# Stacking the high and low parts of a value sum into one 128-partition tile, with one-layer T blocks in 64x128 pairs and filler matmuls

## The chip, the cores and the metric

The kernel runs on one core of one Trainium2 chip. The metric is the device time in microseconds (us), lower is better. Most executions of a kernel agree within 0.3%.

## The reference, cut to what matters

A block A is a recurrent attention: 64 segments of 32 tokens, and 8 memory rows that each segment hands to the next. A block B is a gated feed-forward layer. The model is A, B, A, B with the same weights both times.

```python
for s in range(n_seg):                                   # 64 segments, one after another
    h = concat([mem, xs])                                # 8 memory rows + 32 tokens = 40 rows of 448
    q, k, v = h @ Wq, h @ Wk, h @ Wv                     # 16 heads of 256
    p = softmax(where(mask, q @ k.T / 16, -1e9))
    o = sum_over_heads((p @ v) @ Wo)
    mem = o[:8]                                          # the next segment waits for this
    outs.append(o[8:])
...
x = x + A(layernorm(x)); x = x + B(layernorm(x))         # twice
```

## The kernel before

The kernel folds Wq with Wk and Wv with Wo, so that a segment is: T = M h (the "T blocks"), scores, softmax, U = h p, and the value sum N U. The two A layers run side by side, the second four steps behind the first: steps 0 to 3 and 64 to 67 have one layer (40 columns), steps 4 to 63 have two (80 columns). The memory rows go first through every stage: `s_mem` (scores of the memory rows), `p_t_mem` (transpose of their probabilities, tile Pm), `u_mem` (tile UTm), `un_mem` (value sum, 56 matmuls of 448 columns), `m_t` and `m_nat` (the new memory, selected out of the sum). `s_seg`, `u_seg` and `un` do the same for the 32 tokens, `b_layer` and `b_down` are the block B. A list scheduler with tuned numbers (`SLOT`, `BIAS`) puts all operations in order before the kernel is built.

`un_mem` leaves four partial sums, one in each quarter of 32 partitions. The sum over the quarters and the choice of rows are done by one matmul with a 0/1 matrix. The matmul takes bf16, so the sum is split into a high and a low part, each multiplied by the same matrix:

```python
# un_mem, after its 56 matmuls into the PSUM bank C
S.act(... S.hi[:, :] = C)                                 # bf16
S.dve(... S.lo[:, :] = C - S.hi)
# m_t: the new memory, transposed; 4 column blocks x (hi, lo) = 8 matmuls
[MM(C.b()[:, c*16:c*16+16], x[:, w:w+128], S.selm[...], start=(i == 0), stop=(i == 1))
 for c, w in ((0, 0), (1, 128), (2, 256), (3, 320)) for i, x in enumerate((S.hi, S.lo))]
# m_nat: the same in natural layout; 2 matmuls of 448 columns
[MM(C.b()[:, 0:D], S.seln[:, w, :], x[:, :], start=(i == 0), stop=(i == 1)) for i, x in enumerate((S.hi, S.lo))]
```

The first part of each T block has a contraction of 64 rows. It is done in quads of 64x64 matmuls that run side by side (`mode=3`), 25 quads a step:

```python
for o, x in ((0, a), (0, b), (1, a), (1, b)):             # 4 matmuls of 64x64
    h, g = slice(64*side, 64*side+64), slice(64*o, 64*o+64)
    out.append(MM(R[x].b()[g, j*n:j*n+n], S.M3[h, slot, g], mov(3, h), start=(j == 0), stop=False))
```

Of the kernel before, what the change touches and what calls it, by code (L numbers as in the profile page):

```python
# [44 lines left out]
class _Sched:  # L45
# [118 lines left out]
    "t_block@a": 1812, "t_blockm+": -9357, "t_blocks+": -8, "s_mem+": -142986, "p_t_mem@a": 31328, "p_t_mem+": -7192,  # L164
    "u_mem@a": 13521, "u_mem+": 747, "un_mem@a": -12628, "un_mem+": -15687, "un_memh+": -12449, "m_t@a": 6986,
    "m_t+": 6465, "m_tk+": -7932, "s_seg@a": 8100, "s_seg+": -15857, "seg_pt+": -131, "u_seg@a": 3317,
    "u_seg0+": -34358, "u_seg1+": -19122, "u_seg2+": 20412, "u_seg3+": 10778, "m_nat@a": 16787, "m_nat+": 67952,
    "t_block0f+": 11522, "t_block0r+": -14766, "t_block1r+": 16356, "ln_a+": 2229, "ln_ac+": -36153, "un@a": 57889,
    "un+": -5801, "ln_b+": -22707, "b_layer@a": -6365, "b_layer+": 479, "b_down@a": -28772, "b_down+": -16128,
    "m_natx+": 65420, "m_nat@z": -27634, "s_mem@z": 9161, "p_t_mem@z": -19432, "u_mem@z": -334, "un_mem@z": 8381,  # L170
    "m_t@z": 18252, "s_seg@z": -4933, "u_seg@z": 6743, "un@z": -14160, "b_layer@z": 39068, "b_down@z": -1631,
    "seg_pt@z": -26944, "ln_b@z": 196, "stay": 33066, "win": 142,
# [5 lines left out]
    "t_block0f.0@0": 23150, "t_block0r.0@0": 20466, "t_block0r.1@0": 10373, "t_block0r.2@0": -118963,  # L178
    "t_block0r.3@0": -102813, "t_block0r.4@0": -15176, "t_block0r.5@0": 95232, "t_block1f.0@0": 88326,
    "t_block1r.0@0": 70572, "t_block1r.1@0": -90708, "t_block1r.2@0": -669, "t_block1r.3@0": 23477,  # L180
    "t_block2r.0@0": 105637, "s_mem.0@0": -153732, "p_t_mem.0@0": -26811, "u_mem.0@0": -7044, "un_mem.0@0": 68017,
    "m_t.0@0": -385871, "s_seg.0@0": 180805, "u_seg0.0@0": 16616, "u_seg1.0@0": -3087, "u_seg2.0@0": 182854,
    "u_seg3.0@0": -7016, "m_nat.0@1": 15351, "t_block0f.0@1": -101435, "t_block0r.0@1": 175650,
    "t_block0r.1@1": -16550, "t_block0r.2@1": -78417, "t_block0r.3@1": -96693, "t_block0r.4@1": -96697,
    "t_block0r.5@1": -76748, "t_block1f.0@1": 94756, "t_block1r.0@1": -93576, "t_block1r.1@1": -61388,
    "t_block1r.2@1": 13060, "t_block1r.3@1": 192482, "t_block2r.0@1": 98249, "s_mem.0@1": 6005,
    "p_t_mem.0@1": -100695, "u_mem.0@1": 172343, "un_mem.0@1": 413220, "m_t.0@1": 76060, "s_seg.0@1": 89640,
    "u_seg0.0@1": 96587, "u_seg1.0@1": -148969, "u_seg2.0@1": 71131, "u_seg3.0@1": -99947, "un0.0@1": 269897,
    "un0.1@1": -174852, "un0.2@1": 156565, "un0.3@1": -89383, "un1.0@1": 70834, "un1.1@1": 69072, "un1.2@1": -29917,
    "un1.3@1": 26881, "un2.0@1": -89787, "un2.1@1": -86447, "un2.2@1": -10845, "un2.3@1": 13517, "un3.0@1": 89653,  # L190
    "un3.1@1": 89684, "b_layerf.0@1": 94811, "b_layer.0@1": 48867, "b_layer.1@1": 96741, "b_layerf.1@1": 109098,
    "b_layer.2@1": -3240, "b_layer.3@1": 70642, "b_down.0@1": 354372, "b_down.1@1": 72900, "b_down.2@1": 254015,
    "b_down.3@1": 240246, "b_down.4@1": 326259, "b_down.5@1": 354136, "b_down.6@1": 78849, "m_nat.0@2": 168132,
    "t_block0f.0@2": -10118, "t_block0r.0@2": -98052, "t_block0r.1@2": -41109, "t_block0r.2@2": 66134,
    "t_block0r.3@2": 13073, "t_block0r.4@2": -14618, "t_block0r.5@2": -188807, "t_block1f.0@2": -3221,
    "t_block1r.0@2": -1996, "t_block1r.1@2": -186700, "t_block1r.2@2": 70640, "t_block1r.3@2": -74211,
    "t_block2r.0@2": 16205, "s_mem.0@2": -92464, "p_t_mem.0@2": -20075, "u_mem.0@2": -252353, "un_mem.0@2": -101434,
    "m_t.0@2": 84256, "s_seg.0@2": 96377, "u_seg0.0@2": 90135, "u_seg1.0@2": 97804, "u_seg2.0@2": 182858,
    "u_seg3.0@2": 260389, "m_nat.0@3": 151329, "t_block0f.0@3": -2977, "t_block0r.0@3": -188538,
    "t_block0r.1@3": 75914, "t_block0r.2@3": -96292, "t_block0r.3@3": 6194, "t_block0r.4@3": -75085,  # L200
    "t_block0r.5@3": 69297, "t_block1f.0@3": -185930, "t_block1r.0@3": 111423, "t_block1r.1@3": -36939,
    "t_block1r.2@3": 10926, "t_block1r.3@3": 370, "t_block2r.0@3": 12228, "s_mem.0@3": -124071, "p_t_mem.0@3": 180760,
    "u_mem.0@3": 6506, "un_mem.0@3": 65274, "m_t.0@3": -389, "s_seg.0@3": -12148, "u_seg0.0@3": -75151,
    "u_seg1.0@3": 176089, "u_seg2.0@3": 78879, "u_seg3.0@3": 340369, "un0.0@3": -161383, "un0.1@3": -95386,
    "un0.2@3": 323286, "un0.3@3": 5996, "un1.0@3": 11452, "un1.1@3": 76963, "un1.2@3": -93171, "un1.3@3": -179086,
    "un2.0@3": 162572, "un2.1@3": -2533, "un2.2@3": -15402, "un2.3@3": 334269, "un3.0@3": -77062, "un3.1@3": 94056,
    "b_layerf.0@3": 350365, "b_layer.0@3": 277881, "b_layer.1@3": 268897, "b_layerf.1@3": 354905,
    "b_layer.2@3": 181729, "b_layer.3@3": 192495, "b_down.0@3": 101118, "b_down.1@3": 346959, "b_down.2@3": -2948,
    "b_down.3@3": -287771, "b_down.4@3": 93426, "b_down.5@3": 159732, "b_down.6@3": 83157, "m_nat.0@0": -484,
    "un0.4@3": -268098, "un0.5@3": -13365, "un0.6@3": 248971, "un0.7@3": -102719, "un1.4@3": 260089, "un1.5@3": -4388,  # L210
    "un1.6@3": -67736, "un1.7@3": -9258, "un2.4@3": 265064, "un2.5@3": 334268, "un2.6@3": 332162, "un2.7@3": 163179,
    "un3.2@3": 8603, "un3.3@3": -7565, "b_layer.4@3": -10753, "b_layer.5@3": 79668, "b_layer.6@3": 131945,
    "b_layer.7@3": 253283, "b_layer.4@1": 182601, "b_layer.5@1": 61111, "b_layer.6@1": 10905, "b_layer.7@1": -174890,
    "seg_pt.0@3": -162209, "un.0@3": 195399, "ln_b.0@1": 303926,
# [3 lines left out]
def bias_keys(o):  # L218
    if not o.cat:
        return []  # L220
    if o.kind != "pe":
        return [o.cat + o.sub + "+"]
    return [o.cat + "@a"] if o.t < LAG else [o.cat + "@z"] if o.t >= NSEG else []
# [19 lines left out]
class _Order:  # L243
# [13 lines left out]
    def add(self, kind, eng, cost, fn, rd, wr, name=None, mode=0, lat=None, alt=None, base=(0, 0)):  # L257
        o = _Op()
        o.kind, o.eng, o.cost, o.fn, o.rd, o.wr, o.name, o.mode = kind, eng, cost, fn, list(rd), list(wr), name, mode
        o.alt, o.base = alt, base  # L260
        o.succs, o.np, o.alloc, o.fixed, o.lat, o.cat, o.sub, o.t = [], 0, [], None, lat, self.cat, self.sub, self.t
        o.slot = None
        if kind == "pe" and o.cat:
            name = o.cat + o.sub
            i = self.count[name] = self.count.get(name, -1) + 1
            o.slot = f"{name}.{i}@{o.t % 4}"
        self.ops.append(o)
        return o
# [195 lines left out]
def MM(out, lhsT, rhs, **kw):  # L464
    return (out, lhsT, rhs, kw)


class _Kernel:
# [16 lines left out]
    def alloc(self):  # L485
# [37 lines left out]
        self.lo = self.sb("lo", [128, D])  # L523
        self.ident = self.sb("ident", [128, 128])
# [369 lines left out]
    def warm(self, n, rd, wr):  # L894

        S = self
        T = S.tile("R", 1)
        S.mm(lambda: [MM(T.b()[:, 0:512], S.ident[:, :], S.N[:, 0:2, 0:256], start=True, stop=True) for _ in range(n)], n * S.pitch(512), rd, T.res() + wr)
# [6 lines left out]
    def t_block(self, t, units):  # L905
# [14 lines left out]
        def first():  # L920
            out = []
            for a, b in zip(range(0, len(units), 2), range(1, len(units), 2)):
                for j in range(units[a][2]):
                    for o, x in ((0, a), (0, b), (1, a), (1, b)):
                        c, u0, m = units[x]
                        side, slot = S.PLACE[16 * c + u0 + j]
                        h, g = slice(64 * side, 64 * side + 64), slice(64 * o, 64 * o + 64)
# [3 lines left out]
        if pair:  # L931
            S.mm(first, sum(u[2] for u in units[::2]) * S.pitch(n) + 25.0, rd, [r for x in R for r in x.res()] + [k for u in units for k in keys(*u)], mode=3)
# [46 lines left out]
    def s_mem(self, t):  # L979
# [7 lines left out]
             [("TTm",) + k for k in S.TKEYS] + [("hTx", pp, s, l) for l in range(l0, l1)] + S.mkeys(pp, s, l0, l1), C.res())  # L987
# [13 lines left out]
    def s_seg(self, t):  # L1001
# [5 lines left out]
        def mms():  # L1007
            b = G.b()
            out = []
            for l in range(l0, l1):  # L1010
# [9 lines left out]
             [("mask", 0), ("TTsz", 0), ("TTsz", 1)] + S.mkeys(pp, s, l0, l1), G.res())  # L1020
# [19 lines left out]
    def seg_pt(self, t):  # L1040
        S = self
        if t == NSTEP - 1:

            T = S.pe_transpose([("Ps",)], lambda a: S.Ps[:, a, :], [("PTs",)])
# [5 lines left out]
    def p_t_mem(self, t):  # L1050
# [3 lines left out]
        S.mm(lambda: [MM(pT()[:, 0:128], S.Pm[:, :], S.ident[:, :], is_transpose=True)], 60.0, [("Pm",), ("ident",)], C.res() + [("PTm",)])  # L1054
# [12 lines left out]
    def u_mem(self, t):  # L1067
# [6 lines left out]
             [r for l in C for r in C[l].res()] + [("UTm", S.win(t), l) for l in C], mode=3)  # L1074
# [291 lines left out]
```

## Time and profile before

| | before |
|---|---|
| time | 1564.83 us, median of 3 runs (1560.64 to 1566.0) |
| TensorE busy | 96% of the span |
| steps 0 to 3 with the setup, up to the last matmul of their last `un_mem` | 141.7 us |
| steps 4 to 7 | 80.6 us |
| steps 8 to 63, called the middle: 14 periods of four steps | 1236.3 us |
| the rest, called the end | 105.3 us |

From the page of the profiled execution: the span, the busy time of each engine, the clock that TensorE was granted in 40 slices (9 is 90% or more), and the queue that brings instructions (packets, MB, share).

```profile
span 1563.9 us, 81992 instructions
...
PE 1505.9 (96%) x37969; PEld 1106.3 (71%) x37969; DVE 868.0 (56%) x2353; ACT 858.3 (55%) x2599; POOL 112.0 (7%) x259
...
PEclk9989999999999999999999999999999999999998
...
q8 instruction: 298, 4.88, 1.3%
```

The table of the four stretches (length, busy time of each engine with its number of instructions, granted clock, DMA share, GB/s):

```profile
0.00:141.70 141.70, 109.87 (x2060) 64.58 (x2064) 75.43 (x261) 69.72 (x214) 18.96 (x34) 0.93 0.62 147
141.70:222.30 80.60, 76.32 (x2270) 57.10 (x2264) 45.12 (x122) 46.20 (x144) 6.00 (x15) 1.00 0.09 18
222.30:1458.60 1236.30, 1224.48 (x31145) 919.97 (x31136) 696.47 (x1821) 705.36 (x2116) 81.15 (x196) 1.00 0.09 18
1458.60:1563.90 105.30, 95.21 (x2513) 64.61 (x2505) 51.01 (x150) 37.02 (x127) 5.86 (x14) 0.94 0.09 16
```

In the middle TensorE is busy 1224.5 of 1236.3 us at full clock. The two ends have idle time and a clock below 1. What TensorE waited for from 216 to 1440 us, which is the window of all such tables of the middle below (total us, times, longest):

```profile
PE b L138 <- ACT big L798: 4.9, 14, 0.4
PE b L138 <- DVE UTm L799: 3.4, 13, 0.3
PE b L138 <- issue: 2.6, 5, 1.1
```

"issue" is time in which the engine waited for nothing that the profile shows. The timeline of TensorE around one `un_mem` of every fourth step (start, us, engine, line, operation, count, idle before it):

```profile
305.82 0.22 PE L138 MATMUL b<-ident,Pm 128*128 128x128 bf16 x1
305.87 0.92 PE L138 MATMUL b<-big,hB 128*128 128x448 bf16 x4
306.72 0.39 PE L138 MATMUL b<-PTm,hK 40*64 40x128 bf16 x16
307.05 0.55 PE L138 MATMUL b<-big,hB 128*128 128x448 bf16 x2
307.86 2.83 PE L138 MATMUL b<-Nw,UTm 128*32 128x448 bf16 x56 [0.26 <-DVE UTm L799]
```

Between the products for the memory (PTm) and `un_mem` (UTm) two copies of 0.6 us have to happen. They run side by side, one on ScalarE and one on VectorE (307.17 to 307.80 us). Two `b_down` matmuls cover most of that; the rest is the 0.26 us of waiting. The selection of one step (start, us, engine, line, operation, count):

```profile
579.13 0.17 PE L138 MATMUL b<-selm,hi 128*128 128x16 bf16 x1
579.16 0.17 PE L138 MATMUL b<-selm,lo 128*128 128x16 bf16 x1
...
579.52 0.35 PE L138 MATMUL b<-lo,seln 128*128 128x448 bf16 x1
579.71 2.43 PE L138 MATMUL b<-Nw,big 128*128 128x448 bf16 x12
```

The starts show the cost: eight selm matmuls from 579.13 to 579.34 (0.21 us), two seln matmuls from 579.34 to 579.71 (0.37 us). In half of the steps each of these matmuls is cut into four quarters (128x32); there the selection is 32 + 8 matmuls.

### The profile page before, as it was taken

The page shows a single profiled execution, that of the slowest core. Times are in us where ns is not written, and L with a number is a line of the kernel's source. Part 1 is how long each engine was busy: PE and PEld are TensorE (multiplying, and loading weights), DVE is VectorE, ACT ScalarE, POOL GpSimd, SP SyncE. Part 2 cuts the span into 40 slices and gives each one's busy share as a digit, 9 for nine tenths or more (in the row PEclk, how much of TensorE's full clock was granted, in tenths as well). Part 3 has the DMA queues.
Part 4 walks back from the last instruction along what each step waited for, and adds up shares of the span by engine and source line. Part 5 has one row for each costly group of instructions (what it writes and reads, how often), then busy time and mean ns, then how long its engine had stood idle before and what let it go on. Part 6 is the DMA issues. An engine that isn't in the chain of part 4 may idle for free.

```text
span 1563.9 us, 81992 instructions
## 1 busy us (share of the span) xinstructions
PE 1505.9 (96%) x37969; PEld 1106.3 (71%) x37969; DVE 868.0 (56%) x2353; ACT 858.3 (55%) x2599; POOL 112.0 (7%) x259
## 2 busy tenths in 40 slices
PE   5889999999999999999999999999999999999997
PEld 2457667777677777777677777777677777777665
DVE  7434565655555655555555655555564655555554
ACT  5734555655555565655555565555555555555432
POOL 4000000000000000000000000000000000000000
PEclk9989999999999999999999999999999999999998
DMA  8841001000010100000011100101010100000000
GB/s 182 205 117 35 19 18 20 18 17 16 20 20 12 25 15 20 17 15 20 16 20 15 24 15 16 19 16 21 16 21 14 22 18 15 15 18 19 15 19 14
DMA packets 129735, 46.01 MB, mean 29 GB/s; under 512 B 117736, under 2 KB 129264, under 8 KB 129392
## 3 DMA queue, kind: packets, MB, share of 16 engines
q1 hardware_dynamic: 129040, 40.53, 12.4%
q8 instruction: 298, 4.88, 1.3%
q14 instruction: 45, 0.37, 0.1%
q10 hardware_dynamic: 352, 0.24, 0.1%
HBM read 10.33 MB, written 1.84 MB: 8 GB/s over the span
## 4 chain that ended last, share of the span: by engine, by line
PE 92%; DVE 3%; SPq 2%; ACT 2%; issue 1%; DMA 1%; POOL 0%; POOLq 0%; DVEq 0%
PE b L138 92%; SPq L622 2%; ACT hi L1096 1%; ACT big L798 1%; DVE UTm L799 1%; DMA Nw<-in_A_Wo_dram 0%; DVE selm L658 0%; DMA PTs<-Ps 0%; DVE seln L661 0%; DVE stat L845 0%; DVE part L1192 0%; DVE lo L1097 0%; ACT UTm L798 0%; DVE big L799 0%; DVE xn L852 0%
## 5 line engine op out<-in xcount | busy, mean ns | idle before, releaser
L138 PE MATMUL b<-hT,Mw 128*128 128x80 bf16 (+1 forms) x11424 | 436.7, 200 | 9.2 <-issue 8.6
L138 PEld LDWEIGHTS b<-hT,Mw 128*128 128x128 bf16 x11424 | 415.3, 100 | 22.7 <-issue 14.3
L138 PE MATMUL b<-Nw,big 128*32 128x448 bf16 (+1 forms) x3540 | 295.1, 356 | 1.8 <-DVE big L799 0.8
L798 ACT ACTIVATE TTs<-b 128x320 bf16<-128x320 f32 (+5 forms) x658 | 278.4, 426 | 3.7 <-PE b L138 3.7
L798 ACT ACTIVATE TTm<-b 128x80 bf16<-128x80 f32 (+5 forms) x658 | 153.2, 235 | 137.7 <-PE b L138 131.9
L138 PEld LDWEIGHTS b<-Nw,big 128*32 128x32 bf16 (+1 forms) x3540 | 136.4, 97 | 108.8 <-issue 2.4
L138 PE MATMUL b<-xBT,big 128*128 128x128 bf16 (+3 forms) x4900 | 208.7, 215 | 0.7 <-ACT xBT L798 0.7
L138 PEld LDWEIGHTS b<-xBT,big 128*128 128x128 bf16 (+1 forms) x4900 | 187.6, 102 | 19.3 <-issue 7.1
L138 PE MATMUL b<-Nw,UTm 128*32 128x448 bf16 x3752 | 193.5, 358 | 5.3 <-DVE UTm L799 3.6
L138 PEld LDWEIGHTS b<-Nw,UTm 128*32 128x32 bf16 x3752 | 97.2, 98 | 91.2 <-DVE UTm L799 10.0
L798 ACT ACTIVATE big<-b 128x512 bf16<-128x512 f32 (+1 forms) x258 | 128.5, 560 | 35.2 <-PE b L138 35.0
L799 DVE CAST TTm<-b 64x64 bf16<-64x64 f32 (+4 forms) x226 | 48.6, 216 | 176.3 <-PE b L138 174.7
L138 PE MATMUL b<-hT,M 64*64 64x80 bf16 (+2 forms) x7208 | 142.8, 198 | 2.0 <-DVE M L799 1.2
L138 PEld LDWEIGHTS b<-hT,M 64*64 64x64 bf16 (+1 forms) x7208 | 110.9, 108 | 28.0 <-ACT hT L798 7.1
L799 POOL COPY hK<-xn 32x448 bf16<-32x448 bf16 x136 | 75.1, 552 | 657.3 <-DVE xn L852 651.0
L798 ACT ACTIVATE UTm<-b 128x512 bf16<-128x512 f32 (+1 forms) x144 | 78.3, 567 | 74.3 <-PE b L138 74.3
L1263 ACT ACTIVATE gT<-b 128x512 bf16<-128x512 f32 (+2 forms) x128 | 69.4, 542 | 62.1 <-PE b L138 50.2
L138 PE MATMUL b<-big,hB 128*128 128x448 bf16 (+1 forms) x574 | 100.1, 354 | 0.7 <-DVE hB L1264 0.7
L1264 DVE TENSOR_TENSOR hB<-gT,b 128x512 bf16<-128x512 bf16 (+2 forms) x128 | 79.3, 619 | 38.1 <-ACT gT L1263 21.8
L798 ACT ACTIVATE hT<-b 64x16 bf16<-64x16 f32 (+1 forms) x134 | 24.0, 179 | 125.9 <-DVE hT L799 88.0
L799 DVE CAST TTs<-b 64x256 bf16<-64x256 f32 (+4 forms) x226 | 90.5, 401 | 2.7 <-PE b L138 2.6
L1096 ACT ACTIVATE hi<-b 128x448 bf16<-128x448 f32 x67 | 36.5, 544 | 91.6 <-PE b L138 91.6
(112 smaller groups left out, 1625.4 us busy)
## 6 DMA issues: line engine op xcount, KB each, us to landing
big<-in_A_Wo_dram SPq DMA_DIRECT2D x3, 896.0 KB, 6.0
out_dram<-ys SPq DMA_DIRECT2D x32, 56.0 KB, 2.0
big<-in_B_W_up_dram SPq DMA_DIRECT2D x7, 224.0 KB, 2.9
big<-in_B_W_gate_dram SPq DMA_DIRECT2D x7, 224.0 KB, 3.3
big<-in_B_W_down_dram SPq DMA_DIRECT2D x7, 224.0 KB, 2.6
XA<-in_A_x_dram SPq DMA_DIRECT2D x28, 56.0 KB, 2.3
PTs<-Ps SPq DMA_TRANSPOSE x67, 2.4
Nw<-in_A_Wo_dram SPq DMA_DIRECT2D x1, 896.0 KB, 6.1
```

Source lines behind the costliest of these rows:

```text
L138: ins = E.matmul(out, lhsT=lhsT, rhs=rhs, **kw)
L622: S.q.add("dma", ("sp",), {"sp": 6200.0 if w == "Wv" and q else 4100.0}, lambda E: E.dma_start_transpose(out=st[w, q], in_=src[w][:, q * 1 ...
L798: return E.activation(out(), src(), ACT.Copy)
L799: return E.tensor_copy(out(), src())
L1096: S.act(lambda E: E.activation(S.hi[:, :], C.b()[:, 0:D], ACT.Copy), D, C.res(), [("hi",)])
L1263: S.act(lambda E, g=g, R=R, n=n: E.activation(S.gT[:, g, 0:n], R[0].b()[:, 0:n], ACT.Relu), n, R[0].res(), [("gT", g)])
L1264: S.dve(lambda E, g=g, R=R, n=n, fcs=fcs: E.tensor_tensor(S.hB[:, fcs[0]:fcs[-1] + 1, 0:w], S.gT[:, g, 0:n].rearrange("p (a b) -> p a b", ...
```

## The change

Three things, and with them a new tuning of the scheduler:

1. In the steps with two layers, the quarters are added in pairs first (64 partitions), and high and low then stand in one tile of 128 partitions. The selection matrix has the same rows four times, so one pass sums both: half the selection matmuls.
2. In the steps with one layer, two 64x128 matmuls replace each quad of 64x64 (the code says so; the change's own short name speaks of 128x64).
3. Filler matmuls on constant data in the softmax gaps of steps 0, 1 and 67, so that the clock doesn't fall.

```diff
+        if S.stacked(t):                                   # LAG <= t < NSEG: steps 4 to 63
+            S.cp(sumA[:, :] <- C.b()[64:128, 0:D], eng=("act",))
+            S.dve(sumB = C.b()[0:64, 0:D] + sumA)
+            S.cp(S.hi[0:64, :] <- sumB, eng=("act",))
+            S.dve(S.hi[64:128, :] = sumB - S.hi[0:64, :])
+            return
         S.act(... S.hi[:, :] = C)
         S.dve(... S.lo[:, :] = C - S.hi)
 ...
-  for i, x in enumerate((S.hi, S.lo))                      # m_t and m_nat
+  for i, x in enumerate(S.parts(t))                        # (hi,) where stacked
 ...
-                    for o, x in ((0, a), (0, b), (1, a), (1, b)):
+                    for o, x in ((0, a), (0, b), (1, a), (1, b)) if l1 - l0 == 2 else ((-1, a), (-1, b)):
 ...
+    def fill(self, t, n):
+        if t < 2 or t == NSTEP - 1:
+            for _ in range(n):
+                S.warm(2, [("gap", t)], [("filled", t)])    # 2 matmuls of 512 columns
 ...
-    "t_blockm+": -9357, "s_mem+": -142986, ...              # BIAS and SLOT, all new;
-            o.slot = f"{name}.{i}@{o.t % 4}"                # the first and last steps have slots of their own
+            o.slot = f"{name}.{i}@" + (f"a{o.t}" if o.t < LAG else f"z{o.t - NSEG}" if o.t >= NSEG else str(o.t % 4))
```

The new tuning also puts products of the value weights into the softmax gaps of step 0.

## The prediction

> **What bounds it now.** TensorE. The page gives it 96% of the span busy, DVE 56%, ACT 55%; the chain of waits puts 92% on the matmul line. The middle repeats every four steps: in the chain un_mem begins at 307.86, 395.85, 483.82 us, a period of 88.0 us, and the table by stretches shows PE busy 87.4 of 88.0 us at clock 1.00. Some periods have short "issue" gaps (0.3 to 1.1 us); the mean of fourteen is 88.3. The two ends are different: clock 0.81, 0.83, 0.62 in 79 to 107 us and 0.80 after 1536; un_mem takes 4.1 and 5.25 us there against 2.86; and PE waits on softmax (1.08 us, twice) and on "issue" (1.49, 1.38, 0.70, 0.82, 0.84).
>
> **Removed in the middle.** The PE timeline shows the hi/lo selection as 0.21 us (selm) plus 0.37 us (seln) per step. Stacking halves both: about 0.29 us per step, 60 steps, 17.5 us. A mode change costs 95 ns (131 ns start to start against 36); the built order has 744 of them against 796, part of that in the ends. The Trainium skill (TensorEngine Tiling, Key Properties) says that a mode change drains the array; the trace agrees. Summing the built order with start-to-start times of the trace, I estimate 1.4 us less PE work per period.
>
> **Added.** Hi/lo is now ACT, DVE, ACT, DVE instead of ACT, DVE: with 0.54 and 0.62 us each, un_mem's end to the selection goes from about 1.5 to about 2.75 us. The new order puts 2.8 to 3.3 us of other PE work there (before: 1.3 to 4.5), so the latency is just hidden; I allow 0.2 us per period for short stalls where ACT or DVE is in use. The added 1.2 us per step is off the critical chain. Net: 88.3 to about 87.0, fourteen periods, about 17 us.
>
> **Ends.** One-layer T blocks: a quad of 64x64 tiles with 40 columns takes 32 ns, a pair of 64x128 perhaps 28, so about 1 us directly; 400 fewer matmuls should also shorten the issue gaps. Fillers and value-weight products moved into the softmax gaps of steps 0 and 1 keep the clock up. The Trainium skill (TensorE: Matmul & The Clock Gate, Part 1) gives windows of 3.4 us that halve the clock after idleness; the clock column agrees. At full clock un_mem of steps 0 and 1 saves 3.6 us, the last steps about 4. Eighteen more filler matmuls cost 3.9 us, mostly in idle time. I expect about 8 us at the start and 6 at the end, less certain than the middle.
>
> **Sum.** 17 + 8 + 6, rounded down: 1535 us, range 1524 to 1549. Faster by over 2% (below 1533.5) 0.45, within 2% 0.52, slower 0.03.
>
> **Right or wrong, by the profile.** Period 86.7 to 87.4 us, every selection one pass (selm about 0.11, seln 0.19 us); no wait of PE on the lo operation above 0.3 us in the middle; un_mem of steps 0 and 1 near 2.9 us; clock about 1.0 in the first steps and near 1536; ACT and DVE up by about 33 to 37 us each, harmless.
>
> **What would make it wrong.** ACT or DVE queues late at the longer chain, so that PE waits 0.5 us or more per step and the middle gains nothing; PSUM banks held longer because the sum reads them through two engines; fillers that run at half clock and delay the transposes behind them; issue gaps that don't shrink, or that come elsewhere since instruction supply is the limit.

## The result

| | before | after |
|---|---|---|
| time, median | 1562.74 us (4 runs, 1558.9 to 1566.0) | 1542.06 us (4 runs, 1540.84 to 1542.92) |
| ratio | | 0.9868, 95% interval 0.9841 to 0.9895 |
| setup and steps 0 to 3 | 141.7 | 124.8 |
| steps 4 to 7 | 80.6 | 89.6 |
| middle | 1236.3 | 1231.0 |
| end | 105.3 | 95.4 |

A ratio is the mean time of one kernel's runs over that of the other's of the same rounds, so it is not quite the ratio of the medians. The change is worth 1.3%, inside the 2% that count as "the same". The stretches are read from the two traces (spans 1563.9 and 1540.8 us). The page after:

```profile
span 1540.8 us, 79677 instructions
...
PE 1478.4 (96%) x36772; PEld 1084.9 (70%) x36777; DVE 919.9 (60%) x2445; ACT 882.9 (57%) x2627; POOL 111.8 (7%) x259
...
q8 instruction: 288, 4.72, 1.3%
```

The four stretches after:

```profile
0.00:124.80 124.80, 102.83 (x1893) 62.13 (x1900) 75.39 (x267) 67.88 (x208) 19.04 (x34) 1.00 0.73 167
124.80:214.40 89.60, 81.06 (x2263) 61.10 (x2255) 49.13 (x134) 46.77 (x143) 8.50 (x20) 0.92 0.09 18
214.40:1445.40 1231.00, 1206.23 (x30360) 899.45 (x30352) 743.66 (x1888) 732.01 (x2156) 78.58 (x191) 1.00 0.08 18
1445.40:1540.80 95.40, 88.28 (x2276) 62.27 (x2270) 51.72 (x158) 36.24 (x121) 5.71 (x14) 1.00 0.08 17
```

Read the third line against its twin before: TensorE's busy time in the middle fell by 18.3 us (1224.5 to 1206.2), about the 1.4 us a period (19.6 us) that was predicted for the removed work, but the middle became only 5.3 us shorter. So 13 us of removed work turned into waiting (idle time 11.8 before, 24.8 us after). The waits of TensorE in the middle name it:

```profile
PE b L138 <- ACT UTm L865: 15.8, 13, 1.2
PE b L138 <- DVE big L866: 5.1, 14, 0.4
```

The wait of `un_mem` for UTm grew from 3.4 to 15.8 us, once in every period, 1.2 us each time (a fourteenth lies just past the window). The timeline around one of them, with ScalarE (ACT) and VectorE (DVE):

```profile
559.40 1.67 PE L138 MATMUL b<-big,hB 128*128 128x448 bf16 x8
561.04 0.23 PE L138 MATMUL b<-ident,Pm 128*128 128x128 bf16 x1
561.10 0.54 PE L138 MATMUL b<-big,hB 128*128 128x448 bf16 x2
561.57 0.41 PE L138 MATMUL b<-PTs,hK 40*64 40x512 bf16 x4
561.81 0.37 PE L138 MATMUL b<-PTm,hK 40*64 40x128 bf16 x16
562.01 0.39 PE L138 MATMUL b<-PTs,hK 40*64 40x512 bf16 x4
562.03 1.52 ACT L865 ACTIVATE UTm<-b 128x512 bf16<-128x512 f32 x3 [0.46 <-PE b L138]
...
563.61 2.83 PE L138 MATMUL b<-Nw,UTm 128*32 128x448 bf16 x56 [1.21 <-ACT UTm L865]
```

In the new order two products of the previous segment (PTs) stand on TensorE just around the memory's product (PTm). Their copies and the memory's copy all go into the tile UTm, three of them on ScalarE, one behind the other from 562.03 to 563.55. `un_mem` reads UTm, so it waits for the third. (The memory's other copy is on VectorE and was done at 562.95.) Before, `b_down` matmuls stood there, and each engine had one copy to make.

The selection after is one pass, as intended: four selm matmuls in 0.10 us (16 quarters in one step of four), one seln matmul of about 0.19 us:

```profile
570.10 0.25 PE L138 MATMUL b<-selm,hi 128*128 128x16 bf16 x4
...
570.58 0.35 PE L138 MATMUL b<-hi,seln 128*128 128x448 bf16 x1
```

### The profile page after: what moved, and what is told of

It is laid out like the page before. It is cut to its first block, busy times and chain, and to the rows that moved or that the text cites. A ratio compares the mean times of both kernels' runs of the same rounds, so it can differ in the third digit from the quotient of the medians.

```text
span 1540.8 us, 79677 instructions
## 1 busy us (share of the span) xinstructions
PE 1478.4 (96%) x36772; PEld 1084.9 (70%) x36777; DVE 919.9 (60%) x2445; ACT 882.9 (57%) x2627; POOL 111.8 (7%) x259
## 4 chain that ended last, share of the span: by engine, by line
PE 87%; DVE 6%; ACT 4%; DMA 2%; issue 1%; POOL 0%; POOLq 0%
PE b L138 87%; DMA xBT<-xn 2%; ACT UTm L865 2%; DVE big L866 1%; DVE hi L1180 1%; DVE sumB L1178 1%; ACT sumA L865 1%; ACT Mw L865 1%; ACT hi L865 1%; DMA big<-in_A_Wo_dram 0%; DVE xn L919 0%; DVE selm L725 0%; DVE seln L728 0%; DVE stat L912 0%; ACT M L865 0%
## 5 line engine op out<-in xcount | busy, mean ns | idle before, releaser
L865 ACT ACTIVATE TTs<-b 128x320 bf16<-128x320 f32 (+4 forms) x649 | 272.6, 422 | 0.7 <-PE b L138 0.6
L865 ACT ACTIVATE TTm<-b 128x80 bf16<-128x80 f32 (+4 forms) x649 | 150.2, 234 | 166.8 <-PE b L138 162.0
L866 DVE CAST TTm<-b 64x64 bf16<-64x64 f32 (+3 forms) x235 | 52.0, 222 | 232.1 <-PE b L138 226.6
L138 PEld LDWEIGHTS b<-hT,M 64*64 64x64 bf16 (+2 forms) x6808 | 110.8, 107 | 22.2 <-issue 7.6
L865 ACT ACTIVATE UTm<-b 128x512 bf16<-128x512 f32 (+2 forms) x159 | 82.7, 551 | 43.4 <-PE b L138 42.6
L866 DVE CAST big<-b 128x512 bf16<-128x512 f32 (+1 forms) x160 | 93.0, 597 | 11.2 <-PE b L138 10.6
L866 DVE CAST TTs<-b 64x256 bf16<-64x256 f32 (+3 forms) x235 | 97.2, 414 | 0.1
L138 PE MATMUL b<-big,hB 128*32 128x448 bf16 (+1 forms) x742 | 96.6, 353 | 0.0
L865 ACT ACTIVATE sumA<-b 64x448 f32<-64x448 f32 x60 | 32.4, 540 | 101.6 <-PE b L138 101.6
L138 PE MATMUL b<-PTs,hK 40*64 40x512 bf16 (+1 forms) x1024 | 81.8, 362 | 6.3 <-DVE big L866 5.1
```

The lines of the kernel that those rows point to most:

```text
L138: ins = E.matmul(out, lhsT=lhsT, rhs=rhs, **kw)
L865: return E.activation(out(), src(), ACT.Copy)
L866: return E.tensor_copy(out(), src())
```

## The experiments

Moving one operation makes the scheduler choose a very different order. So most experiments keep the order of every engine and swap single operations in place, after the order is fixed. Where the order is meant to change, it is said. All runs were correct. Each ratio is to runs of the kernel before in the same rounds. The table gives the result of each; the stretches are from the profiled execution.

| run | time, us | ratio to before, 95% interval | to step 3 | 4 to 7 | middle | end |
|---|---|---|---|---|---|---|
| after | 1542.06 | 0.9868 [0.9841, 0.9895] | 124.8 | 89.6 | 1231.0 | 95.4 |
| x_nostack | 1558.40 | 0.9971 [0.9945, 0.9996] | 126.3 | 89.4 | 1245.6 | 95.0 |
| x_oldstack | 1592.89 | 1.0190 [1.0165, 1.0216] | 137.4 | 88.3 | 1260.2 | 102.5 |
| x_quads | 1558.66 | 0.9972 [0.9951, 0.9994] | 130.0 | 89.7 | 1237.9 | 98.4 |
| x_nofill | 1541.74 | 0.9864 [0.9840, 0.9888] | 126.2 | 89.5 | 1230.5 | 94.5 |
| x_stack8 | 1553.28 | 0.9926 [0.9904, 0.9947] | 126.7 | 89.2 | 1240.3 | 95.6 |
| x_fill57 | 1541.84 | 0.9854 [0.9835, 0.9874] | 127.2 | 85.7 | 1232.6 | 95.1 |
| x_pad | 1551.37 | 0.9922 [0.9898, 0.9945] | 127.6 | 87.8 | 1238.5 | 94.8 |
| x_early | 1548.04 | 0.9892 [0.9871, 0.9913] | 125.8 | 90.2 | 1232.5 | 94.7 |
| x_pad128 | 1545.58 | 0.9881 [0.9860, 0.9902] | 130.3 | 88.6 | 1231.8 | 94.4 |
| x_pairs | 1542.51 | 0.9865 [0.9846, 0.9884] | 124.6 | 89.6 | 1231.6 | 94.9 |
| x_early2 | 1537.77 | 0.9843 [0.9822, 0.9865] | 125.8 | 89.7 | 1225.2 | 94.9 |
| x_best | 1535.83 | 0.9830 [0.9803, 0.9857] | 124.8 | 85.2 | 1227.6 | 95.9 |

### x_nostack: the change without the stack, in the same order

```diff
-  S.cp(sumA ...); S.dve(sumB ...); S.cp(S.hi[0:64] ...); S.dve(S.hi[64:128] ...)
+  S.act(S.hi[:, :] = C); S.dve(S.lo[:, :] = C - S.hi)      # in the places of the first two
-  for i, x in enumerate((S.hi,))
+  for i, x in enumerate((S.hi, S.lo))
```

> The changed kernel with the hi/lo stack taken out again and every engine's order kept: two selection passes, and ACT, DVE instead of ACT, DVE, ACT, DVE. Theory A: the stack saves its 0.29 us of PE work per step, and the middle gained little only because the new order has a wait of its own (un_mem of every fourth step waits 1.2 us for ACT copies), which has nothing to do with the stack. Then the period goes from 87.75 to about 88.9 us, the time to about 1558 us, and the 1.2 us wait stays. Theory B: the longer chain eats its own gain. Then the period stays within 0.3 us of 87.75 and the time within 4 us of 1542.

The time rose by 16 us, to 1558.40. The shortest period rose from 87.73 to 88.65 us, and the wait for UTm stayed:

```profile
PE b L138 <- ACT UTm L866: 15.8, 13, 1.2
```

So within this order the stack is worth the work that it removes (TensorE's busy time in the middle is 1221.7 us without it, 1206.2 with it), and its longer latency costs about 0.9 us in the whole middle (idle time 23.9 us without it, 24.8 with it). The wait for UTm belongs to the order and not to the stack. The table shows one thing more: without the stack the middle of the new order takes 1245.6 us, 9.3 more than that of the order before. So the new order is slower by itself, by its waits (idle time 11.8 us before, 23.9 here), and the stack has to pay for that first.

### x_oldstack: the stack alone, in the order before

```diff
-  S.act(S.hi[:, :] = C); S.dve(S.lo[:, :] = C - S.hi)
+  S.act(sumA = C[64:128]); S.dve(sumB = C[0:64] + sumA)
+  S.act(S.hi[0:64] = sumB); S.dve(S.hi[64:128] = sumB - S.hi[0:64])
```

> The kernel before with the stack alone, in the order of before on every engine. The chain needs about 2.75 us from the end of un_mem, and that order has 1.3 to 1.5 us of PE work there in two of four steps. If the latency counts where no work covers it: PE waits about 1.25 us twice per period, less 1.16 us of selection saved, period about 89.3 us, time about 1580 us. If the latency is harmless: period about 86.8 us, time about 1547 us.

The kernel became 1.9% slower than before. The waits of TensorE in the middle show why:

```profile
PE b L138 <- DVE hi L1114: 29.1, 27, 1.1
PE b L138 <- ACT big L801: 6.6, 14, 0.5
```

27 times, in about every second step, the selection stood too soon after `un_mem` and waited up to 1.1 us for the fourth operation of the chain. In this order the stack doesn't pay; it needs one that puts other work there. The new tuning isn't decoration: it is the condition of the change. One part stays open: TensorE's busy time in the middle fell by only 8.6 us here (1224.5 to 1215.9), about half of what the removed passes take.

### x_quads: quads of 64x64 again in the one-layer steps

```diff
-  for o, x in ((0, a), (0, b), (1, a), (1, b)) if l1 - l0 == 2 else ((-1, a), (-1, b)):
+  for o, x in ((0, a), (0, b), (1, a), (1, b)):
```

> The changed kernel with the one-layer T blocks in 64x64 quads again, order kept. If the pairs are worth only their PE time (4 ns a quad) : 1 us slower. If 400 fewer matmuls also feed the queue better: 2 to 5 us slower, with longer issue gaps in the steps 0 to 3 and 64 to 67. Middle the same, 87.75 us.

Far more was lost than expected: 16.6 us. In steps 0 to 3 of the two traces, successive pairs with 40 columns start 25 ns apart and successive quads 32 ns; with 25 a step and eight such steps the direct difference is 1.4 us, about as thought. But steps 0 to 3 lost 5.2 us (the clock was also at half from 85.4 us for 3.4 us), the end 3.0, and the middle 6.9, although its instructions are the same in both kernels. The waits of TensorE from 70 to 216 us in x_quads begin with:

```profile
PE b L138 <- issue: 5.3, 7, 1.4
```

In the kernel after, "issue" is 1.8 us in that window, in two waits. One of the seven, in the timeline:

```profile
84.37 0.20 PE L138 MATMUL b<-hT,M 64*64 64x40 bf16 x1 [1.44 <-issue]
```

It stands in the middle of the quads. So instructions, not data, were late. And the loss in the middle must come from something that the 200 more matmuls ahead of it shift. That gave the two runs with padding, below.

### x_nofill: the change without fillers

```diff
+        if self.cat.startswith("fill"):
+            o.over = lambda x: []                           # emitted as nothing
```

> The changed kernel without fillers, order kept. If the fillers keep the clock up: clock under 0.9 again in the steps 0 to 2 or near the end, un_mem of step 0 or 1 over 4 us, 3 to 8 us slower. If the products moved into those gaps already do it: the same time within 1.5 us, clock 1.00.

The time is the same (1541.74 against 1542.06). Without fillers the clock falls twice in step 1, for 3.4 us each, and the `un_mem` of that step takes 4.51 us instead of 2.83. (One of the two falls, at 78.2 us, is also in x_early2, which has the fillers.) The total doesn't show it: the fillers add nothing that can be measured. In step 0 the clock stays up without them; that this is due to the value-weight products which the new order puts there is likely, but no run takes them away.

### x_stack8 and x_fill57: why steps 4 to 7 became longer

These steps went from 80.6 to 89.6 us, which the prediction did not see. The table of stretches above gives one reason: the clock there is 0.92. Two runs, one for each theory (the edit of x_stack8 is shown by what it does):

```diff
 # x_stack8
-  return LAG <= t < NSEG
+  return 8 <= t < NSEG        # hi and lo in two tiles in steps 4 to 7; same order
 # x_fill57: in steps 5 and 7, on the bank of the operation that follows
+  5 x MM(C.b()[:, 0:512], S.ident, S.M[:, 0, 0:4, :])      # ahead of p_t_mem
+  3 x the same                                              # ahead of un_mem
```

> The kernel after, with the stacked hi and lo used only from step 8 on; steps 4 to 7 take the old hi and lo in two tiles. All other operations and their order stay. In the kernel after, the stretch from un_mem of step 3 to that of step 7 takes 89.6 us against 80.6 before. Theory 'latency': the longer chain to hi and lo (about 1.2 us more per step) is exposed there, because these steps have little other work; then the stretch shrinks by 2 to 4 us and the time is about 1538 to 1540 us. Rival 'clock': the loss is the half clock that follows the softmax gaps of these steps (un_mem takes 5.42 and 4.27 us there against 2.83); then the stretch keeps its length within 1 us and the time stays at 1541 to 1543.

> The kernel after, with eight more filler matmuls of 512 columns in steps 5 and 7 (five ahead of the transpose of the memory's probabilities, three ahead of un_mem), all else in the same order. Theory 'clock': the clock stays at 1.00 in the stretch from step 3 to step 7, un_mem of steps 5 and 7 takes 2.8 us again, the stretch shrinks by 3 to 5 us and the time is about 1538 us. Rival, after the run without fillers, which lost nothing: the fillers cost what they save, so the clock is repaired and the time stays within 1 us of 1542.

Without the stack steps 4 to 7 keep their length (89.2), so in this order latency isn't most of what they lost. A smaller part isn't excluded: the second pass puts about 1 us of matmuls back, and in x_oldstack, the stack in the order before, the same stretch takes 88.3 us with 5.5 us of waits for hi. (The middle of x_stack8 lost 9 us, so that neither theory had its time right; it has 62 matmuls more up to step 8, and the padding runs below show what such a shift can do.) With the fillers they fall to 85.7 us:

```profile
127.20:212.90 85.70, 80.74 (x2279) 59.67 (x2271) 49.24 (x134) 46.66 (x143) 8.53 (x20) 0.98 0.11 19
```

The clock goes from 0.92 to 0.98. So about 3.9 of the 9.0 us were the clock; x_best repeats it (85.2). A shift of the instruction stream moves this stretch too (87.8 us in x_pad, 88.6 in x_pad128, at clocks of 0.96 and 0.94), so the share is good to some 2 us. The two tables of stretches divide the 9.0 us in another way: TensorE is busy 4.7 us longer (76.3 to 81.1), and idle 4.3 us longer (4.3 to 8.5), now mostly for the softmax's result and the copies behind it (Pm 2.8 us, UTm 1.9), for which it hardly waited before. Why these come later in the new order stays open. In the timed runs of x_fill57 the gain doesn't show beyond the interval (ratio 0.9854 against 0.9868), so that the time is the one that the rival forecast; in its profiled execution the setup took 2.4 us and the middle 1.6 us longer.

### x_pad and x_pad128: the place of the instruction stream

200 or 128 tiny matmuls are put at the very start, where TensorE has nothing to do; everything behind them is the same.

```diff
+  n x MM(T.b()[:, 0:8], S.ident[:, :], S.ident[:, 0:8], start=True, stop=True)   # n = 200, later n = 128
   MM(... transposes of the first memory ...)
```

> The kernel after, with 200 tiny matmuls (128x128 weights, 8 columns) ahead of the first transposes, where the TensorE has nothing to do; this is as many matmuls as the 64x64 quads added before the middle. All else is identical. Theory 'place': the 6.9 us that the quads cost in the middle, whose instructions were the same, come from where the instruction stream lies, so that the same shift by 200 matmuls costs the same: the middle is about 1238 us instead of 1231, with extra time at the same place of each period. Rival: the shift alone does nothing, the middle stays within 1.5 us of 1231, and the quads' loss in the middle has another cause. In both the start may be up to 5 us longer by the matmuls themselves.

> As the run with 200 tiny matmuls at the start, but with 128. The trace shows that the TensorE's instructions come in packets of 16384 bytes, 288 of them for 73889 recorded TensorE instructions, so 256 instructions or 128 matmuls a packet, and that two packets never start less than 3.3 us apart. 200 matmuls shift every later instruction by one packet and 144 instructions, 128 matmuls by one packet exactly. Theory 'place in the packet': the middle is at 1231 us within 1.5 us, as in the kernel after, without the stalls of 0.3 to 0.7 us behind the T blocks that 200 matmuls brought. Rival 'any shift costs', or the matmuls' own time: the middle is at 1235 us or more.

With 200 the middle went from 1231.0 to 1238.5 us, as with the quads. With 128 it is 1231.8. The start of x_pad128 was 5.5 us longer up to step 3, 3.8 us of that in one wait for a transfer of xBT, whose cause I did not look for; if the other executions had it too, it covers the 3.5 us by which its time, 1545.58 us, is longer. The waits of TensorE in the middle of x_pad:

```profile
PE b L138 <- ACT UTm L867: 15.8, 13, 1.2
PE b L138 <- DVE big L868: 5.1, 14, 0.4
PE b L138 <- issue: 2.3, 6, 0.5
```

and of x_pad128, where "issue" is gone:

```profile
PE b L138 <- ACT UTm L867: 15.8, 13, 1.2
PE b L138 <- DVE big L868: 5.1, 14, 0.4
PE b L138 <- DMA xBT<-xn: 1.5, 4, 0.4
PE b L138 <- DVE sumB L1193: 0.5, 1, 0.5
```

The Trainium skill (Runtime: NRT & Kernel Launch, Instruction fetch mechanics) says that instructions are refilled in blocks of 16 KiB, 256 instructions, and the trace agrees: 288 packets of 16384 bytes for 73889 recorded TensorE instructions. 128 matmuls with their weight loads are exactly one block, 200 are a block and 144 instructions. So the place within the block matters, and not the shift as such. Waits are only half of the 7.5 us: in the middle of x_pad TensorE's idle time rose by 3.7 us and its busy time, for the same matmuls, by 3.8.

The traces show it more directly. I counted the recorded TensorE instructions (matmuls, weight loads and about 340 semaphore and drain instructions between them) and took the remainder by 256 at each "issue" wait after the first 60 us:

```
traces: 14 (before, after and the twelve experiments)
"issue" waits after 60 us: 100, of 0.16 to 1.50 us, 61.4 us together
remainder by 256 at the wait: 189 to 194, in all 100
```

Every such wait lies at one place of the block. Most crossings cost nothing: the kernel after has 288 packets and 5 such waits. In x_pad, in the period that begins behind the `un_mem` of step 23, crossings lie at matmuls 694 and 822, and against the kernel after it loses 0.13 us at 696 and 0.64 us at 824: in and behind the T block, where matmuls are short. A period has 2168 matmuls, with the few other recorded instructions nearly 17 blocks, so the places move by only 1 to 2 matmuls a period and a loss comes again: x_pad is longer in each of the fourteen. In the kernel before a period has 2224 matmuls, and the places wander.

Two things in my own expectations fall. I had begun to read the 3.3 us between packets as a limit of supply; x_pairs (next) has 200 matmuls less a period and gains nothing, so the rate of supply does not bind the middle of the kernel after. And what TensorE waits for at the crossing isn't shown. It is not the next packet, which starts only 1.0 us or more after the wait ends. The packet before is the better candidate: in all 100 waits it had ended 1.19 to 1.60 us before the wait ended, while over all crossings after 60 us the median is 3.0 us. This fits a packet that came late; no run tests it.

### x_pairs: pairs of 64x128 in the two-layer steps too

```diff
-  for o, x in ((0, a), (0, b), (1, a), (1, b)) if l1 - l0 == 2 else ((-1, a), (-1, b)):
+  for o, x in ((-1, a), (-1, b)):
```

> The kernel after, with pairs of 64x128 matmuls in the steps of two layers as well (80 columns) instead of quads of 64x64, all operations in the same order: 50 matmuls less in each step, 200 of 2168 in a period of four steps. In the trace a quad of 64x64 takes 4 x 12.1 = 48 ns in those steps; a pair of 64x128 with 40 columns takes 2 x 17.6 = 35 ns against 43 for a quad. Theory 'supply and rate': a pair takes 36 to 40 ns, so 25 of them a step save about 0.25 us, a period 1 us, and the supply of instructions is easier by 400 in 4336, so that the short slow-downs behind the T blocks go: the period is 86.6 to 87.0 us, the time about 1526 to 1530 us. Rival: at 80 columns the two halves of a pair do not run side by side with full-width outputs, a pair takes about 72 ns, and the time is 1560 us or more; or what un_mem waits for (UTm, four steps apart) takes up what is saved, and the time stays at 1538 or more.

Nothing was gained. With 80 columns successive pairs start 36 ns apart, and so do successive quads. (The 48, 43 and 35 ns in the expectation were means over a whole group and had the mode change ahead of the group in them.) The pairs' advantage of the one-layer steps isn't there.

### x_early and x_early2: the wait for UTm taken away

The order of one step in four is changed, from step 11 on. The segment products 1 and 0 move forward, right behind the segment's scores, and `b_down` matmuls move to the place between the memory's product and `un_mem`:

```diff
-  s_seg, b_down x4, p_t_mem, b_down, u_seg1, u_mem, u_seg0, un_mem            # TensorE
+  s_seg, u_seg1, u_seg0, b_down x2, p_t_mem, b_down, u_mem, b_down x2, un_mem
-  PTm, UTm(u_seg1), UTm(u_seg0), UTm(u_mem), big(u_seg1)                      # ScalarE
+  UTm(u_seg1), ..., PTm, UTm(u_seg0), UTm(u_mem), big(u_seg1)
```

> The kernel after, with the order of one step in four changed from step 11 on: the segment products 1 and 0 of the step before stand on the TensorE right behind the segment's scores instead of around the transpose of the memory's probabilities, two of the five b_down pairs stand behind the memory products, and the copies that un_mem needs come first on ScalarE. No work is added or taken away (one or two mode changes at most). Theory 'wait': the middle gained 5 us instead of 17 because un_mem of every fourth step waits 1.2 us for the copies into UTm; then that wait falls to 0.3 to 0.5 us, the period from 87.9 to about 87.2 us and the time to about 1532 to 1534 us. Rival 'moved': ScalarE and VectorE are full there, the wait comes back on another operation (Pm, PTs, hi), and the time stays at 1540 or more.

> The run with the early segment products, mended: the copies into UTm of those two products now come first (the first try took the wrong ones of the pairs forward, so un_mem waited 0.7 us for the last copy on VectorE), and the b_down matmuls are not cut into quarters, so that a period has 2168 matmuls as in the kernel after. Theory 'wait': un_mem of every fourth step waits at most 0.4 us for UTm, the period is about 87.1 to 87.3 us and the time about 1533 to 1536 us. Rival 'moved': the wait comes back elsewhere and the time is 1540 or more.

x_early failed by my mistake: it moved the copies of the other layer forward, and `un_mem` still waited 0.7 us, now for VectorE. It also cut two matmul pairs into quarters, 12 matmuls more a period. x_early2 mends both. Its waits in the middle:

```profile
PE b L138 <- DVE big L969: 6.1, 14, 0.5
PE b L138 <- DVE UTm L969: 2.1, 10, 0.2
PE b L138 <- DMA xBT<-xn: 1.0, 4, 0.3
PE b L138 <- ACT big L968: 0.9, 4, 0.2
```

The same place in its timeline:

```profile
560.37 0.63 PE L138 MATMUL b<-PTs,hK 40*64 40x512 bf16 x8
560.93 0.93 PE L138 MATMUL b<-big,hB 128*128 128x448 bf16 x4
...
562.83 0.93 PE L138 MATMUL b<-big,hB 128*128 128x448 bf16 x4
563.97 2.83 PE L138 MATMUL b<-Nw,UTm 128*32 128x448 bf16 x56 [0.21 <-DVE UTm L969]
```

The wait for UTm fell from 15.8 to 2.1 us, the middle from 1231.0 to 1225.2 us, the time to 1537.77. That is the mechanism, but at half its size: 1.0 us less waiting a period, 0.41 us less period (mean 87.93 to 87.51). The traces say where the rest went: over the middle TensorE's idle time fell by 12.2 us, but its busy time rose by 6.4 (1206.2 to 1212.7) with the same matmuls. Three more mode changes a period account for some 0.29 us of it (an estimate, 95 ns each), and the wait for "big" is some 0.1 us longer. In the timed runs the gain isn't clear of the noise: the intervals of x_early2 and of the kernel after overlap, and one of its four runs took 1542.61 us. Also, the transpose of Pm still begins 2.7 us after the memory's scores in both kernels (558.31 to 561.04, and 559.19 to 561.91), so the softmax itself sets how early the rest can be.

### x_best: three of these together

> Three edits of earlier runs together on the kernel after: the early segment products (mended), the eight fillers of steps 5 and 7, and pairs of 64x128 in all steps. From the traces: the early products took 5.8 us off the middle (1225.2 against 1231.0), the fillers 3.9 us off the stretch from step 3 to step 7 (85.7 against 89.6); the pairs alone changed nothing, but they take 400 of 4336 TensorE instructions out of each period and so should keep the other two edits from losing time to the supply of instructions. If these effects add: the middle at 1225, the stretch at 86, and the time at 1532 to 1536 us. Rival: the fillers are worth nothing in the timed runs, as the two earlier runs on fillers suggest; then the time is that of the early products alone, 1537 to 1539 us.

1535.83 us, ratio 0.9830: better than both kernels, 0.38% of the time before (6 us) below the kernel after by the ratios. The intervals of these two overlap a little (0.9857 against 0.9841), but their runs don't: 1533.69 to 1537.39 against 1540.84 to 1542.92 us. The time lies in the range expected if the effects add. Steps 4 to 7 keep the fillers' gain (85.2). The middle keeps most of that of the early products (1227.6 against 1225.2); new waits for the transfer of PTs, 3.1 us in all, take the rest. The intervals of x_early2 and x_best overlap, so how much the fillers add in the timed runs isn't settled.

## Why the prediction was right or wrong

The time fell into the range: 1535 us predicted, 1542.06 measured, range 1524 to 1549. The sum came out better than its terms, and that was luck: the middle gave 5.3 us instead of 17, the end 9.9 instead of 6, and the start's 7.9 for 8 is 16.9 gained in steps 0 to 3 less 9.0 lost in steps 4 to 7.

- **"Stacking halves both: about 0.29 us per step", "1.4 us less PE work per period": right.** Busy time of the middle fell by 18.3 us, 1.3 us a period, and x_nostack puts 14.6 us back into the middle.
- **"Net: 88.3 to about 87.0, fourteen periods, about 17 us": wrong, this is the step that failed.** It measured 5.3 us (88.3 to 87.93). The allowance of "0.2 us per period for short stalls" was the mis-sized term: the wait for UTm alone grew from 0.26 to 1.21 us a period. I had looked for stalls on the new chain (hi and lo) and found that the order covers it, which is right. But the order was new everywhere, and it moved other operations in front of another consumer, `un_mem`. x_nostack shows that this wait isn't the stack's, x_early2 that it can be had back, at half.
- **"the latency is just hidden": right for this order**, and x_oldstack shows that it isn't so in the order before (29.1 us of waiting, 1.9% slower). The added work itself fell otherwise than thought: VectorE rose by 51.9 and ScalarE by 24.6 us, where 33 to 37 each were expected.
- **"Fillers ... keep the clock up", "About 8 us at the start and 6 at the end": 7.9 is near by luck, 9.9 is more, and the reasons hold only partly.** `un_mem` of steps 0 and 1 takes 2.83 us as predicted, but without the fillers the time is the same. Of the 16.9 us in steps 0 to 3 and the 9.9 at the end, x_quads puts 5.2 and 3.0 back; the rest came with the new order, and no run takes it apart.
- **"about 1 us directly; 400 fewer matmuls should also shorten the issue gaps": the direction was right, the size missing.** Direct 1.4 us; with the issue gaps 16.6 us, of which 6.9 in the middle are due to the place of the same instructions in the blocks.
- Not foreseen: steps 4 to 7, +9 us; about 3.9 us of it is the clock, why the rest is lost is open.

## What to carry to other kernels

When a change comes with a new order, check every consumer on the recurrent chain in the new order, and not only the operations that the change adds: removed work becomes time only if the next wait isn't already standing there. Count TensorE instructions and not only their time: short matmuls are where crossings of an instruction block show, and a shift of the same stream by half a block moved this kernel by 0.5%. So before believing a gain or loss of that size, shift the stream by padding and look again.

## What the Trainium skill lacked or had wrong

- Runtime: NRT & Kernel Launch, Instruction fetch mechanics, calls the cost of crossing a 16 KiB boundary "mostly hidden". Mostly, yes (5 waits for 288 packets in the kernel after). But all 100 "issue" waits of 14 traces lie at one place of the 256-instruction block (remainder 189 to 194), up to 1.5 us each, and shifting the stream by 144 instructions cost 7.5 us in the middle, by 256 only 0.8.
- TensorEngine Tiling (Array Packing), Key Properties, says that a mode change drains the array, without a duration. Here it costs 95 ns between the quads of the T block and the full matmuls behind them (131 ns start to start against 36); the kernel after has 744 mode changes in all.
- TensorE: Matmul & The Clock Gate, Measured speedup vs the span model, gives the span of one pack (the duration of one matmul and about 4 ns for each further tile), but not how soon the next pack of the same kind can start. Here, with 80 columns, successive packs of both kinds start 36 ns apart. That is what the page's Back-to-back issue gap gives for a single matmul: N / 2.4 + 2.5 ns, by our estimate 35.8 ns for N = 80. With 40 columns it is 25 ns for pairs of 64x128, the same section's floor for a single matmul, and 32 ns for quads of 64x64.
